# A gated mix of linear-memory attention and a SwiGLU layer on one core: seven weight operands made in four pieces, and loads, splits and two down groups on other beats

## The chip, the core and the metric

The kernel runs on one core of a Trainium2 chip. The metric is the device time of one execution in microseconds (us). Three runs before the change gave 1719.92, 1721.14 and 1722.72, with a median of 1721.14. TensorE is called PE below, its weight loads PEld, VectorE DVE, ScalarE ACT, GpSimd POOL, and the engine whose queue issues every DMA SP. Each engine works its own queue in the order in which the program was written. The kernel places every instruction by hand, and no scheduler moves any.

## The reference

```python
x = A_x                                            # 1 x 2048 x 576
g = sigmoid((x * gate_w).sum(-1, keepdims=True))
a = attention_with_memory(x, wq, wk, wv, beta) @ wo  # 32 heads of 18, 4 segments of 512 rows
b = (silu(x @ w_gate) * (x @ w_up)) @ w_down       # 576 -> 4608 -> 576
return g * a + (1 - g) * b
```

In each segment of 512 rows the attention is causal softmax within the segment. It is mixed per head, by `sigmoid(beta)`, with a linear-attention read of a memory that the earlier segments have filled. All inputs and the output are float32.

## The kernel before, in words

**Precision by splitting.** A float32 operand is held as two tiles of the type fp32r. The high one is ACT's copy of the number (an `activation` with `Copy`). The low one is DVE's difference of the number and the high one (`tensor_sub`). A product is then three matmuls: high by high, high by low, low by high. This making of a high and a low is called a split.

**Three stretches of the program.** First, up to about 219 us, the projections q, k, v and the memory. Then the long middle: 72 turns, in which the gate and up products of the feed-forward layer, its down products and the softmax attention are interleaved. Last, from about 1628 us, the output stage: the attention result times `wo`, the gate, and the down groups that are left.

**A turn.** The feed-forward layer is worked in two halves of the rows (two segments each) and 36 tiles of 128 hidden features, so 72 turns (`seq`, the loop over `pos`). In a turn gate and up of one feature tile for 1024 rows are computed as a 2x2 by 2x2 block product with seven multiplications in place of eight (Strassen's scheme, in Winograd's form). The seven products are the calls `seven(t, j)` for j = 0 to 6. Each is six matmuls of 512 columns with a weight operand `ops[j]` and an x operand `XO[j]` (L1027), and one for the last rows of the 576 (L1030). In a product the first two matmuls read the high of the weight operand, the third reads the low.

- Weight operands j = 0, 3 and 6 are plain blocks of the weights (a11, a12, a22). j = 1, 2, 4 and 5 are sums and differences of blocks that POOL makes (`total`, L265).
- After product 2 DVE adds a bank and a row (L1096). After product 4 ACT copies a bank (L1103) and DVE adds (L1104). Then ACT applies silu (L1106 for the first half of the rows, after a load of its table, and L1108 for the second). After product 6 DVE multiplies (L1112 and L1113), and that gives the hidden tile, which is split into `hh` and `hl` for the down product.

**Beats.** Between the products stand eight calls of `tick()`, the beats 0 to 7 of the turn: beat 0 after product 0, and so on, 5 and 6 together after product 5, 7 after product 6. A beat first runs what was put off to it (`due`), then down groups if there are any (`SHARE`), then steps of the attention (`att_gen`). A number of 8 or more in a plan's table is a beat of the next turn: 8 is its beat 0.

**Down groups.** Hidden tiles are taken in threes (`CH`). In each third turn 16 groups of 9 matmuls (L870) are issued, of 320 or 256 columns, two or three in each of the beats 2 to 7, so such a turn takes about 31 us, against about 17 and 12 for the two others.

**Who makes the weight operands.** `w_make(half, f)` plans in turn f - 1 what turn f needs: the sums on POOL, the highs on ACT (`HIGH` gives the beat, L269), the lows on DVE (`LOW`, L272). Each of the seven operands is a tile of its own of 128x512 (high and low, 256 each) from a pool of seven buffers. For the first two turns the operands are also written to DRAM (L275) and fetched again at the start of the second half (`w_fetch`, L713), because the weights are the same.

**The change of halves.** In the last turn of the first half (number 35) and ten further beats (`BREAK`) the x operands of the second half are loaded (`LOADS`), combined on POOL (`SUMS`) and split (`PARTS`) by `x_second`. Four of its eight loads lie in buffers of the weight operands.

**The output stage.** A row tile is transposed, multiplied by `wo` in two column halves (14 matmuls each, `products`, L160), and after each half one down group is issued (`downs(1)`). The first down groups there read the hidden tile of the very last turn.

## Time and profile before

| what | value |
|---|---|
| median of three runs | 1721.14 us |
| the profiled execution's own time | 1722.04 us |
| its span | 1720.3 us |
| PE busy | 1705.2 us (99%) |
| DVE busy | 1362.3 us (79%) |
| ACT busy | 1084.6 us (63%) |
| POOL busy | 937.9 us (55%) |
| granted PE clock | 1.00 |

A timeline row has the start in us from the span's beginning, the duration, the engine, the line, the operation, out<-in, shape and count. In brackets stand the idle time before it and what ended that. A row of the groups has the busy time, the mean duration of one in ns, and the idle time before. A row of the waits has the total, the number and the longest. A row of the windows has the stretch, its length, each engine's busy time with its count, the granted clock, the DMA share and GB/s. Matmuls of 512 columns are shown with 0.39 us each, but in a run of them one starts every 0.23 us (six in 1.52 us), since they overlap. DVE's instructions overlap by about 0.08 us in the same way.

### The profile page before, as it was taken

The numbers are of one execution on the slowest core, as the hardware profiler recorded it, in microseconds if no ns is written. First come the engines' busy times: TensorE is split into PE (matmuls) and PEld (weight loads), VectorE is DVE, ScalarE is ACT, GpSimd is POOL, SyncE is SP. The second block draws the span as 40 slices with busy tenths as digits, with TensorE's granted clock in tenths as the row PEclk, the third lists the DMA queues.
The fourth block names the chain that finished last, engine by engine and source line by source line (L and its number), as shares of the span: only waits on it lengthen the run. The fifth ranks groups of instructions, "written<-read, shape, count | busy, mean of one in ns | idle before, by whom it ended". The sixth has DMA issues, their size and how long they took to land.

```text
span 1720.3 us, 34819 instructions
## 1 busy us (share of the span) xinstructions
PE 1705.2 (99%) x11868; PEld 1479.8 (86%) x11868; DVE 1362.3 (79%) x3231; ACT 1084.6 (63%) x2123; POOL 937.9 (55%) x1194
## 2 busy tenths in 40 slices
PE   9999999999999999999999999999999999999999
PEld 7899978888888888888888788888888888888899
DVE  6557588888888889888889777787787788788655
ACT  7666576775776677567666756665666576566411
POOL 4434546666665655656566555565555555555311
PEclk9999999999999999999999999999999999999999
DMA  8654499998998898997979986787778677767633
GB/s 282 235 186 140 162 310 186 224 228 178 218 230 197 180 216 203 183 209 195 201 159 256 289 172 145 178 183 162 151 180 188 142 164 181 170 131 167 191 120 136
DMA packets 524002, 328.05 MB, mean 191 GB/s; under 512 B 411184, under 2 KB 460336, under 8 KB 523824
## 3 DMA queue, kind: packets, MB, share of 16 engines
q1 hardware_dynamic: 523824, 325.83, 78.0%
q8 instruction: 93, 1.52, 0.4%
q14 instruction: 85, 0.70, 0.1%
HBM read 165.76 MB, written 76.09 MB: 141 GB/s over the span
## 4 chain that ended last, share of the span: by engine, by line
PE 84%; DVE 7%; ACT 3%; issue 2%; DMA 2%; POOL 1%; SPq 0%; DVEq 0%; ACTq 0%; POOLq 0%
PE bank L1027 33%; PE bank L870 26%; PE bank L160 10%; PE bank L1030 5%; PE bank L728 4%; PE bank L776 2%; PE bank L777 1%; PE bank L415 1%; DVE hl L972 1%; DVE scr L734 1%; PE bank L461 1%; DVE dw L972 1%; DVE p L760 1%; PE bank L351 1%; DVE xo L138 1%
## 5 line engine op out<-in xcount | busy, mean ns | idle before, releaser
L761 POOL TENSOR_TENSOR p<-pe,p 128x512 f16<-128x512 f32 x320 | 378.4, 1182 | 417.0 <-DVE p L760 399.9
L870 PE MATMUL bank<-dw,hh 128*128 128x320 f32 (+1 forms) x2304 | 487.1, 304 | 1.5 <-DVE ya L880 1.5
L870 PEld LDWEIGHTS bank<-dw,hh 128*128 128x128 f32 x2304 | 381.1, 189 | 13.9 <-DVE ya L880 3.3
L746 ACT ACTIVATE pe<-bank,mb 128x512 f32<-128x512 f32 (+3 forms) x512 | 247.9, 526 | 196.2 <-DVE mb L734 183.1
L870 PE MATMUL bank<-dw,hl 128*128 128x320 f32 (+1 forms) x1152 | 340.6, 296 | 1.4 <-DVE hl L138 1.4
L734 DVE CUSTOM_DVE_ANT_0 scr<-bank,cm 128x512 bf16<-128x512 f32 (+3 forms) x512 | 246.5, 481 | 6.8 <-PE bank L728 0.2
L880 DVE TENSOR_TENSOR ya<-bank,ya 128x320 f32<-128x320 f32 x352 | 158.2, 453 | 77.8 <-PE bank L870 77.0
L870 PEld LDWEIGHTS bank<-dw,hl 128*128 128x128 f32 x1152 | 217.9, 189 | 1.9 <-DVE hl L138 1.9
L1030 PE MATMUL bank<-xr,rh 128*128 128x512 f32 x504 | 196.3, 390 | 0.0
L754 POOL TENSOR_SCALAR_AFFINE_SELECT pe<-pe 128x256 f32<-128x256 f32 (+1 forms) x320 | 151.6, 474 | 52.1 <-ACT pe L746 42.6
L760 DVE CAST p<-pe 128x512 f16<-128x512 f32 x320 | 160.6, 502 | 0.0
L265 POOL TENSOR_TENSOR ws<-raw 128x256 f32<-128x256 f32 x140 | 116.3, 831 | 16.1 <-DMA raw<-in_wf_dram 8.4
L728 PE MATMUL bank<-kst,qst 108*128 108x512 bf16 (+3 forms) x512 | 124.6, 305 | 0.3 <-DMA kst<-stk 0.2
L972 DVE TENSOR_TENSOR hl<-row,hh 128x512 fp32r<-128x512 f32 x120 | 108.4, 903 | 8.9 <-ACT hh L971 8.5
L1030 PEld LDWEIGHTS bank<-xr,rh 128*128 128x128 f32 x504 | 94.6, 188 | 20.4
L1104 DVE TENSOR_TENSOR row<-bank,row 128x512 f32<-128x512 f32 x72 | 49.7, 690 | 62.6 <-ACT bank L1103 62.5
L746 ACT ACT_TABLE_LOAD x69 | 88.5, 1283 | 10.8 <-DVE mb L734 9.8
L1089 ACT ACTIVATE bank<-bank 128x512 f32<-128x512 f32 x72 | 41.9, 582 | 79.8 <-PE bank L1030 76.7
L1106 ACT ACT_TABLE_LOAD x71 | 91.1, 1283 | 1.3
L1099 ACT ACTIVATE row<-bank 128x512 f32<-128x512 f32 x72 | 43.2, 600 | 71.5 <-PE bank L1030 71.3
L265 POOL TENSOR_TENSOR ws<-raw,ws 128x256 f32<-128x256 f32 x70 | 58.8, 840 | 49.9 <-DVE wo__22504 L272 9.7
L1103 ACT ACTIVATE bank<-bank 128x512 f32<-128x512 f32 x72 | 42.2, 587 | 65.5 <-PE bank L1030 65.1
(2170 smaller groups left out, 4123.1 us busy)
## 6 DMA issues: line engine op xcount, KB each, us to landing
raw<-in_wf_dram SPq DMA_DIRECT2D x140, 256.0 KB
rh<-rc SPq DMA_DIRECT2D x72, 336.0 KB
dc<-dw SPq DMA_DIRECT2D x36, 576.0 KB
dw<-dc SPq DMA_DIRECT2D x36, 576.0 KB
stk<-q SPq DMA_DIRECT2D x32, 384.0 KB
draw<-in_wd_dram SPq DMA_DIRECT2D x36, 288.0 KB
rc<-rt SPq DMA_DIRECT2D x42, 224.0 KB
vd<-vps SPq DMA_DIRECT2D x8, 912.0 KB
```

Source lines behind the costliest of these rows:

```text
L160: nc.tensor.matmul(t, st[n], mv[n], start=(n == 0), stop=(n == 13))
L265: (nc.gpsimd.tensor_sub if sub else nc.gpsimd.tensor_add)(src[j], p(), q())
L728: nc.tensor.matmul(t[:, c:c + w], qs[:KR, pr, P * i:P * i + P], ks[:KR, pr, 0:w], start=True, stop=True)
L734: nc.vector.tensor_tensor_reduce(scr[:, :w], t[:, c:c + w], cm[:, L - w:L], -SCALE, 3.0e38, OP.add, OP.min, m[:, k:k + 1])
L746: nc.scalar.activation(pe[:, c:c + w], t[:, c:c + w], AF.Exp, bias=m[:, k:k + 1], scale=SCALE)
L754: nc.gpsimd.affine_select(d, d, pattern=pat, compare_op=OP.is_ge, fill=0.0, base=0, channel_multiplier=1)
L760: nc.vector.tensor_copy(p[:, 0], pe)
L761: nc.gpsimd.tensor_sub(p[:, 1], pe, p[:, 0])
L870: nc.tensor.matmul(ts[m], p, q[:, cs], start=(n == 0), stop=(n == 3 * CH - 1))
L880: nc.vector.tensor_add(ya[:, i, cs], t, ya[:, i, cs])
L1027: nc.tensor.matmul(t, w[:, p, z], x[z][:, q], start=first and n == 0, stop=False, skip_group_check=True)
L1030: nc.tensor.matmul(t, rem[:, RPOS[j]], XR[j], start=False, stop=True, skip_group_check=True)
```

## The change

Three things are altered together.

1. The seven weight operands of a turn are made in four pieces: the operands (0, 3) in one tile, (1, 2) in one, (4, 6) in one, and 5 alone (`PAIRS`). A pair has one ACT copy and one DVE difference of 128x512 where there were two of 128x256. Each piece has one buffer, of the same total size as the seven before. The pairs are possible because a11 and a12 lie side by side in the raw tile `g`. The sums 1 and 2 now lie side by side in `ws`, and sum 4 is written over a21, beside a22. The beats of highs and lows are:

| operand | high before | high now | low before | low now | product at |
|---|---|---|---|---|---|
| 0 | 2 | 4 | 5 | 6 | 8 (after beat 7) |
| 3 | 7 | 4 | 8 | 6 | after 10 |
| 1 | 3 | 3 | 6 | 7 | after 8 |
| 2 | 3 | 3 | 7 | 7 | after 9 |
| 4 | 7 | 8 | 9 | 10 | after 11 |
| 6 | 9 | 8 | 11 | 10 | after 14 |
| 5 | 8 | 9 | 10 | 11 | after 12 |

   The copies to and from DRAM go by the same four pieces (512 KB for a pair, 256 KB before for one operand).
2. In `x_second` the loads, sums and splits stand on other beats, and four of the loads lie in `ws` and in the pieces (4, 6) and 5.
3. In the output stage the first two down groups are issued together: both groups' matmuls for the first two hidden tiles, and then both groups' for the last one (`down_parts`).

```diff
-HIGH = (2, 3, 3, 7, 7, 8, 9)
-LOW = (5, 6, 7, 8, 9, 10, 11)
+PAIRS = ((0, 3), (1, 2), (4, 6), (5,))
+HIGH = (4, 3, 8, 9)
+LOW = (6, 7, 10, 11)
...
-PARTS = ((1, 0, 0), (4, 0, 1), (10, 1, 0), (11, 1, 5), (12, 1, 3), (13, 0, 5), (13, 1, 1), (14, 1, 4), (15, 1, 2),
-         (17, 0, 2), (17, 1, 6), (18, 0, 3), (20, 0, 4), (22, 0, 6))
-FIRST = (9, 10, 11, 15, 17, 17, 19)
+PARTS = ((2, 0, 0), (4, 0, 1), (10, 1, 0), (11, 1, 5), (12, 1, 3), (13, 0, 5), (13, 1, 1), (14, 1, 4), (15, 1, 2),
+         (16, 0, 2), (17, 1, 6), (17, 0, 3), (18, 0, 4), (20, 0, 6))
+FIRST = ((9, 10, 18, 15), (4, 3, 8, 6))
...
-        def high(j):
-            ops[j] = op_tile()
-            nc.scalar.activation(ops[j][:, 0], src[j], AF.Copy)
-
-        def low(j):
-            nc.vector.tensor_sub(ops[j][:, 1], src[j], f32(ops[j][:, 0]))
...
+        def high(n):
+            tile_of[n] = op_tile(n)
+            op_views(ops, n, tile_of[n])
+            nc.scalar.activation(halves(n, 0), flat(n), AF.Copy)
+
+        def low(n):
+            nc.vector.tensor_sub(halves(n, 1), flat(n), f32(halves(n, 0)))
...
-        for j in range(7):
-            todo += [(HIGH[j], lambda j=j: high(j)), (LOW[j], lambda j=j: low(j))]
+        for n in range(4):
+            todo += [(HIGH[n], lambda n=n: high(n)), (LOW[n], lambda n=n: low(n))]
             if half == 0 and f < KEPT:
-                todo.append((LEAD + j + 3, lambda j=j: keep(j)))
+                todo.append((LOW[n] + 1, lambda n=n: keep(n)))
...
-                    downs(1)
+                    if n == 1 and hf == 0:
+                        down_parts([groups.pop(0) for _ in range(2)], CH - 1, CH)
+                    else:
+                        downs(1)
```

The queue of DVE at the end of turn 26 (two turns without down groups have gone by), before the change. `wo__10209`, `wo__10239` and `wo__10241` are the operands 0, 1 and 2 of turn 27; `dw` is the split of a down weight.

```order
L272 TENSOR_TENSOR wo__10209<-raw,wo__10209 128x256
L972 TENSOR_TENSOR dw<-draw,dw 128x576
L272 TENSOR_TENSOR wo__10239<-ws,wo__10239 128x256
L1112 TENSOR_TENSOR row<-bank_10250,row 128x512
L1113 TENSOR_TENSOR row<-row 128x512
L272 TENSOR_TENSOR wo__10241<-ws,wo__10241 128x256
L272 TENSOR_TENSOR wo__10299<-raw,wo__10299 128x256
```

The same place now (L997/L998 are the split of before's L971/L972, L1147 and L1148 its L1112 and L1113, L297 the low; `woa` is the pair (0, 3), `wob` the pair (1, 2)):

```order
L998 TENSOR_TENSOR dw<-draw,dw 128x576
L297 TENSOR_TENSOR woa__9946<-raw,woa__9946 128x512
L1147 TENSOR_TENSOR row<-bank_9942,row 128x512
L1148 TENSOR_TENSOR row<-row 128x512
L297 TENSOR_TENSOR wob__9933<-ws,wob__9933 128x512
L139 TENSOR_TENSOR hl<-row,hh 128x512
```

The low of operand 0 now stands behind the split of `dw` and is one instruction with that of operand 3. The low of operand 1 has moved from ahead of the two multiplications to behind them, and is one with that of operand 2. The lows of operands 3 and 4, at the beginning of the next turn, are gone from there.

The queue of ACT between product 3 and the silu of the same turn, before:

```order
L1099 ACTIVATE row<-bank_10145 128x512
L269 ACTIVATE wo__10239<-ws 128x256
L269 ACTIVATE wo__10241<-ws 128x256
L1103 ACTIVATE bank_10250<-bank_10143 128x512
L971 ACTIVATE dw<-draw 128x576
L746 ACTIVATE pe<-bank_10222,mb_2325 128x128
L746 ACTIVATE pe<-bank_10222,mb_2325 128x384
L1106 ACT_TABLE_LOAD
L1106 ACTIVATE row<-row 128x512
```

The same place now (L1138 is the copy of before's L1103, L1141 the silu of its L1106, L772 the exponential of its L746):

```order
L1134 ACTIVATE row<-bank_9844 128x512
L294 ACTIVATE wob__9933<-ws 128x512
L1138 ACTIVATE bank_9942<-bank_9842 128x512
L294 ACTIVATE woa__9946<-raw 128x512
L997 ACTIVATE dw<-draw 128x576
L772 ACTIVATE pe<-bank_9916,mb_2325 128x128
L772 ACTIVATE pe<-bank_9916,mb_2325 128x384
L1141 ACT_TABLE_LOAD
L1141 ACTIVATE row<-row 128x512
```

The high of operand 0 stood earlier in the turn, and now stands, as that of the pair (0, 3), between the copy and the silu.

More of the change, by code (lines that the diff above doesn't have):

```diff
@@ L231, in gated_mix, with op_tile, op_flat, op_home @@
     wraw_of, wops, rhs = {}, {}, []
-    def op_tile():
-        return wop.tile([P, 2, 2, P], F32R, name="wo_")
+    def op_tile(g, shape=None, dtype=F32R):
+        n = len(PAIRS[g])
+        return wop.tile(shape or [P, 2, n, 2, P], dtype, name=f"wo{'abcd'[g]}_", bufs=1)
+    def op_flat(t):
+        return f32(t).rearrange("p a j k n -> p (a j k n)")
+    def op_home(f, g):
+        return wc[f, :, 8 * P * g:8 * P * g + 4 * P * len(PAIRS[g])]
+    def op_views(ops, g, t):
+        for i, j in enumerate(PAIRS[g]):
+            ops[j] = t[:, :, i]
     def r_block(h, o):
@@ L255, in r_fetch, with w_make @@
         nc.sync.dma_start(f32(rhs[f % 2][:96]).rearrange("p j n -> p (j n)"), rc[f // 4, :, f % 4])
-    def w_make(half, f, LOW=LOW):
+    def w_make(half, f):
         g, u = wraw_of.pop(f)
@@ L709, in w_fetch, with one @@
             ops = wops[1, f] = [None] * 7
-            def one(j):
-                ops[j] = op_tile()
-                nc.sync.dma_start(f32(ops[j]).rearrange("p a k n -> p (a k n)"), wc[f, j])
-            return [(j + 2 if f else FIRST[j], lambda j=j: one(j)) for j in range(7)]
+            def one(n):
+                t = op_tile(n)
+                op_views(ops, n, t)
+                nc.sync.dma_start(op_flat(t), op_home(f, n))
+            return [(FIRST[f][n], lambda n=n: one(n)) for n in range(4)]
         kp = pool(ast, "kp", 2, side="right")
@@ L994, in x_second @@
         def x_second(new, rest):
-            r = {}
+            r, pair = {}, []
             todo = []
```

45 lines of the change are left out of this document (32 added, 13 removed).

## The prediction, made before the changed kernel was run

> **What bounds the kernel now.** I read the engines' busy shares first, then two windows (the busy times stand in the order PE, PEld, DVE, ACT, POOL), and then what PE and PEld wait for.
>
> ```profile
> span 1720.3 us, 34819 instructions
> PE 1705.2 (99%) x11868; PEld 1479.8 (86%) x11868; DVE 1362.3 (79%) x3231; ACT 1084.6 (63%) x2123; POOL 937.9 (55%) x1194
> 215.00:845.00 630.00, 624.89 (x4449) 532.74 (x4449) 548.92 (x1319) 428.65 (x838) 386.24 (x517) 1.00 0.92 209
> 960.00:1625.00 665.00, 664.64 (x4716) 574.02 (x4715) 524.38 (x1284) 423.57 (x820) 363.28 (x464) 1.00 0.75 171
> ```
>
> PE is the bound in every stage, at the full clock, and the change takes no matmul from it. What the change can gain is only what PE now waits; what it can lose has no such limit. In the second half of the turns (960 to 1625) PE is idle for 0.4 us of 665: a new wait there is a loss in full. DVE is 87% busy in the first half (548.92 of 630), so work reaches PE from there with little to spare.
>
> ```profile
> PE bank L1027 <- ACT bank L1103: 2.4, 5, 0.9
> PE bank L1027 <- DVE bank L1096: 1.7, 4, 0.7
> PE bank L870 <- DVE hl L138: 1.4, 2, 1.2
> PE bank L1027 <- DVE xo L138: 0.5, 2, 0.3
> PE bank L1027 <- DVE wo__3704 L272: 0.3, 1, 0.3
> PEld bank L1027 <- ACT bank L1103: 6.3, 10, 1.3
> PEld bank L1027 <- DVE bank L1096: 5.0, 9, 1.1
> ```
>
> A wait shows at the weight load and again, shorter, at the matmul. PE waits for the bank that ACT copies (L1103), the bank that DVE adds (L1096), late x and hidden lows (L138), and only once for a weight operand's low (L272). All of it together is some 14 us.
>
> **Part 1, the pairs: what is saved.** The first row is DVE's window for the lows alone, the second ACT's for the highs; the others are the same operation at 512 elements.
>
> ```profile
> 219.20:1628.10 1408.90, 281.64 (x489) 1.00 0.84 193
> 219.20:1628.10 1408.90, 190.30 (x487) 1.00 0.84 193
> L972 DVE TENSOR_TENSOR hl<-row,hh 128x512 fp32r<-128x512 f32 x120 | 108.4, 903 | 8.9 <-ACT hh L971 8.5
> L971 ACT ACTIVATE hh<-row 128x512 fp32r<-128x512 f32 x120 | 75.3, 628 | 0.9 <-DVE row L1113 0.9
> 732.49 0.68 DVE L972 TENSOR_TENSOR hl<-row,hh 128x512 fp32r<-128x512 f32 x1
> ```
>
> A low of 256 takes 281.64/489 = 0.58 us in the mean, a high 190.30/487 = 0.39. Seven lows are 4.03 us a turn; three of 512 (0.90) and one of 256 are 3.29, so DVE saves 0.74 us a turn. ACT goes from 2.74 to 2.27 and saves 0.47. Over some 70 turns that is 52 us of DVE and 33 of ACT, but neither is the bound, so this is worth only the waits that it shortens.
>
> **Part 1: what comes later.** A low must be there at the third matmul of its product, 0.45 us after the first (two starts of 0.23). The pair (1, 2) is now made behind both multiplications, and operand 1 is wanted a product earlier than operand 2 was, which had that place. I take two windows. The first is the end of turn 13, without a split of `dw`; `wo__6442`, `wo__6473` and `wo__6475` are operands 0, 1 and 2.
>
> ```profile
> 488.64 0.39 PE L1030 MATMUL bank<-xr,rh 128*128 128x512 f32 x1
> 490.55 1.46 PE L1027 MATMUL bank<-xo,wo__6473 128*128 128x512 f32 x5
> 489.13 0.69 DVE L1112 TENSOR_TENSOR row<-bank,row 128x512 f32<-128x512 f32 x1 [0.53 <-PE bank L1030]
> 489.74 0.68 DVE L1113 TENSOR_TENSOR row<-row 128x512 f32<-128x512 f32 x1
> 490.34 0.42 DVE L272 TENSOR_TENSOR wo__6475<-ws,wo__6475 128x256 fp32r<-128x256 f32 x1
> 485.69 0.58 ACT L1103 ACTIVATE bank<-bank 128x512 f32<-128x512 f32 x1 [0.44 <-PE bank L1030]
> 488.18 0.63 ACT L1106 ACTIVATE row<-row 128x512 f32<-128x512 f32 x1
> ```
>
> DVE here waits for PE's product 6 (489.03), then multiplies twice. The pair's low begins at 490.34 at the earliest and takes 0.68: ready at 491.02, wanted at 490.55 + 0.45 = 491.00. So even an idle DVE is 0.02 late. But ACT has the high of (0, 3) between L1103 and the silu now: 0.63 less an overlap of 0.1 is 0.52 more. L1103 itself waited for PE, so nothing earlier makes this good; the silu ends at 489.33 in place of 488.81, L1112 starts at about 489.36, and the low is ready at 491.25, 0.25 late. With the mean 0.90 for 512 elements it is 0.47. Bounds 0.02 and 0.47; I take 0.20, near the row's own 0.25, since in some turns ACT has room before the silu.
>
> The second window is the end of turn 26, with the split of `dw` (the place whose order is shown above).
>
> ```profile
> 740.09 1.59 PE L1027 MATMUL bank<-xo,wo__10209 128*128 128x512 f32 x6
> 741.75 1.69 PE L1027 MATMUL bank<-xo,wo__10239 128*128 128x512 f32 x6
> 739.61 0.81 DVE L272 TENSOR_TENSOR wo__10209<-raw,wo__10209 128x256 fp32r<-128x256 f32 x1
> 740.35 0.95 DVE L972 TENSOR_TENSOR dw<-draw,dw 128x576 fp32r<-128x576 f32 x1
> 741.22 0.96 DVE L272 TENSOR_TENSOR wo__10239<-ws,wo__10239 128x256 fp32r<-128x256 f32 x1
> 742.11 0.68 DVE L1112 TENSOR_TENSOR row<-bank,row 128x512 f32<-128x512 f32 x1
> 743.54 0.41 DVE L272 TENSOR_TENSOR wo__10241<-ws,wo__10241 128x256 fp32r<-128x256 f32 x1
> 740.22 0.63 ACT L1106 ACTIVATE row<-row 128x512 f32<-128x512 f32 x1
> ```
>
> DVE works without a gap. Operand 0 falls away at 739.61, `dw` takes its place until 740.48, and the pair (0, 3) is ready at 741.16, wanted at 740.09 + 0.45 = 740.54: 0.62 late. With 0.90 it is 0.84; where DVE arrives 0.4 earlier, by the shorter lows before, it is 0.2. L1112 then starts about 741.1 (also the silu's time, 740.85 and a part of the 0.52), the pair (1, 2) begins 1.2 to 1.4 later and is ready at 743.0 to 743.2, wanted at 742.20 plus the 0.62: another 0.2 to 0.4. Bounds 0.2 and 1.2; I take 0.7.
>
> How many turns: in every third turn the 16 down groups lie between the beats 2 and 7, and the next turn's operands have time. Of the 47 others, 11 in the first half have `dw` in this place, as in the second window (weights' lows are not made again in the second half); 35 count as the first, and the start of the second half is fetched. 35 x 0.20 = 7.0 and 11 x 0.7 = 7.7: **14.7 us**, between 35 x 0.02 + 11 x 0.2 = 2.9 and 35 x 0.47 + 11 x 1.2 = 29.7. What waits behind PE is the next product and all that follows.
>
> The pair (4, 6) and operand 5 come one beat later than 4 and 5 did, and the pair is 0.27 longer than one low. Ahead of them two lows are gone. No row shows these being waited for: 0 to 13 us (0.27 in 47 turns); I take 1.5.
>
> **Part 1: what PE is spared.** L1096 has two lows fewer ahead of it (those of operands 3 and 4, 1.16 us by the mean): of its 5.0 us I take 3.0 as gone, 0 to 5.0. L1103 keeps its 6.3: ahead of it on ACT stand 0.52 in place of two times 0.3, at the same place behind the same sum. I take 0, between 2 gained and 2 lost. In turn 0 the wait comes from a write to DRAM:
>
> ```profile
> 232.96 0.42 ACT L269 ACTIVATE wo__2722<-ws 128x256 fp32r<-128x256 f32 x1 [2.25 <-DMA wc<-wo__2473]
> 227.75 1.17 SPq L275 DMA_DIRECT2D wc<-wo__2473  x1
> ```
>
> ACT may not overwrite operand 2 until the write of 256 KB, issued at 227.75, has landed at 232.96. The pair's write is 512 KB, issued from the same place in SP's queue, and ACT's high of the next pair stands at the same beat, ahead of L1103 again: 0 to 1.5 us more, I take 0.5. SP has fewer issues than before, which were hidden anyway.
>
> **Part 2, x on other beats.**
>
> ```profile
> 912.44 0.69 DVE L138 TENSOR_TENSOR xo<-raw,xo 128x512 fp32r<-128x512 f32 x1 [1.59 <-ACT xo L137]
> 915.35 1.65 PE L1027 MATMUL bank<-xo,wo__12823 128*128 128x512 f32 x6 [0.71 <-DVE bank L1096]
> 951.80 1.43 PE L1027 MATMUL bank<-xo,wo__13331 128*128 128x512 f32 x5 [0.29 <-DVE xo L138]
> 955.51 1.43 PE L1027 MATMUL bank<-xo,wo__13380 128*128 128x512 f32 x5 [0.24 <-DVE xo L138]
> ```
>
> In turn 35 DVE waits 1.59 us for ACT at the first x split, with L1096 queued behind it; the split now stands behind L1096, and that wait of PE goes (counted in the 3.0). The x operands 4 and 6 come one and two beats sooner, so the other two waits, 0.5 us, go. The fetch of pair (4, 6), at beat 18, must wait on SP for a split at beat 17, and everything in SP's queue with it: 0 to 2 us if it lands after product 4 begins; I take 0, since the same pool of operands was issued at the same place before.
>
> **Part 3, two down groups together.**
>
> ```profile
> 1633.06 0.41 PE L870 MATMUL bank<-dw,hl 128*128 128x320 f32 x1 [1.21 <-DVE hl L138]
> 1635.36 0.40 PE L870 MATMUL bank<-dw,hh 128*128 128x256 f32 x2
> 1635.72 0.40 PE L870 MATMUL bank<-dw,hh 128*128 128x256 f32 x2
> ```
>
> Three matmuls of 256 columns take 0.36 us (1635.36 to 1635.72), so six of the second group put 0.7 us of work into the wait of 1.21. Gain 0.7; nothing to lose.
>
> **The sum**, on the profiled execution's 1722.04: 14.7 + 1.5 + 0.5 - 3.0 - 0.5 - 0.7 = 12.5, so 1734.5. That execution lies 0.9 over the median of 1721.14, so the forecast is **1733**, about 0.7% slower.
>
> **Rivals.** *Faster: the saved fixed cost reaches PE.* If DVE is early by the 0.74 us a turn where it matters, so that no pair is late, PE keeps the gains and part of the L1103 waits: 3.0 + 0.5 + 0.7 + 4 = 8 us, 1713, or some 1717 with half of it. For it: DVE is 87% busy in the first half, and the second window's delay is all queue. Against it: the first window has no queue in it, only PE, two multiplications and one low. It decides from a mean lateness under 0.09 us in 47 turns (4.2/47). Chance 0.16. The Trainium skill, page "VectorE: DVE Perf Modes", section on the TRN2 errata, states this rule: an instruction from SBUF pays a fixed latency once, so tiles of 512 and more are to be preferred. By it alone the change would gain; the trace agrees on the price of the instruction (0.68 for 512 against twice 0.42), but what is asked here is when the first half of the pair is ready.
>
> *No change: the two lists cancel.* Lateness of 0.05 to 0.13 in the 47 turns, as an idle DVE with the silu in time would have it: 2.4 to 6 us, less 4.2 gained: 1719 to 1723. Chance 0.14.
>
> *Much slower: DVE meets POOL each time.* The same form of low takes 0.42 and 0.96 in one window. If the pairs stretch like that, the upper bounds hold: 29.7 + 5 - 3 = 32, 1753. For it: the mean of 0.90 in 120 cases. Against it: nearly every window would have to be the worst one. From about 1745 on I give it 0.08.
>
> **How the numbers follow.** The likeliest, slower by its waits at products 0 and 1, has 0.62 and by itself a range of 1726 to 1745. With 0.08 for much slower, slower has 0.70. A measurement of this kernel tells about 0.2% (3.4 us) from no change; the three chances are bounded there. The range for 8 in 10 takes in the even case and the upper edge of the faster: 1717 to 1745.
>
> **What would show it.** In the profile after: PE and PEld waits for L297 (`woa`, `wob`) in most turns of two in three, some 10 to 20 us in all, in the second half too; the wait on L1131 (before's L1096) smaller than 5.0; silu 0.5 later against L1138; the wait at 1633 down to about 0.5; those at 951 and 955 gone. Wrong it is if the pairs (0, 3) and (1, 2) are ready before the third matmul with DVE idle, or if PE's busy time in 960 to 1625 shows no new gap.

## The result, and the profile after

The changed kernel takes 1759.8 us (median of four runs, 1758.5 to 1762.5) against 1721.9 for the kernel before in the same comparison. The ratio is 1.0223, with a 95% interval of 1.0211 to 1.0236. I had forecast 1733, with a range of 1717 to 1745. The sign was right and the size was not: 38 us lost, where I had worked out 12.5.

The head of the page of the profiled execution after (own time 1762.54), and two windows of the turns, with the busy times in the order PE, PEld, DVE, ACT, POOL:

```profile
span 1760.7 us, 34418 instructions
PE 1719.8 (98%) x11868; PEld 1474.9 (84%) x11868; DVE 1308.6 (74%) x3021; ACT 1064.2 (60%) x1913; POOL 938.9 (53%) x1194
215.00:845.00 630.00, 611.56 (x4266) 513.09 (x4265) 508.21 (x1184) 410.26 (x724) 375.31 (x502) 1.00 0.89 204
960.00:1660.00 700.00, 687.73 (x4834) 584.81 (x4832) 511.27 (x1213) 421.24 (x730) 374.59 (x475) 1.00 0.74 169
```

The clock is 1.00 as before, and PE has as many matmuls as before. DVE is 53.7 us less busy (1362.3 before), and yet PE now idles 18.4 us of 630 in the first window (5.1 before) and 12.3 us of 700 in the second (0.4 of 665 before). That is 25 us more. PE's busy time also rose, from 1705.2 to 1719.8 for the same matmuls, so idle time shows only a part of the loss. What PE and PEld wait for, some of the largest rows and that of the bank which DVE adds (L1131, before's L1096):

```profile
PE bank L1062 <- ACT bank L1138: 3.4, 6, 1.3
PE bank L1062 <- DMA woa__13034<-wc: 2.1, 1, 2.1
PE bank L1062 <- DVE wob__22052 L297: 1.6, 1, 1.6
PE bank L1062 <- DVE woa__7348 L297: 1.4, 1, 1.4
PE bank L1062 <- DVE wod__6412 L297: 1.1, 1, 1.1
PEld bank L1062 <- ACT bank L1138: 6.9, 9, 1.7
PEld bank L1062 <- DVE wob__22052 L297: 2.0, 1, 2.0
PEld bank L1062 <- DVE bank L1131: 1.7, 4, 0.8
```

Each late low is a row of its own, since each turn's tile has its own number. Added up over PEld's rows, the lows of (1, 2), `wob`, make PEld wait 24.3 us in 39 turns, operand 5, `wod`, 17.4 in 22, (0, 3), `woa`, 10.4 in 12, and (4, 6), `woc`, 3.1 in 10. Before, the lows had some 2 us between them. The wait for the bank that DVE adds fell from 5.0 to 1.7, the waits for late x at 951 and 955 are gone, and so is that of 1.21 in the output stage.

For what follows I use one more reading. For every two matmuls in a row I take the distance of their starts less the median distance of all pairs of the same two shapes, and add up what exceeds 0.06 us, by the product in which the waiting matmul stands. A part of these sums is there in every kernel; what counts is the difference of two columns. All in us; the names of the versions are explained below. The sums are from one execution each, whose own time stands in the last row.

| PE held up in | before | change | first two lows early | operand 5 early | all lows early | highs and lows earlier |
|---|---|---|---|---|---|---|
| product 0 | 2.9 | 14.1 | 4.2 | 17.2 | 4.0 | 4.3 |
| product 1 | 6.9 | 24.1 | 7.9 | 27.3 | 8.7 | 8.7 |
| product 5 | 5.2 | 18.9 | 20.7 | 5.2 | 5.2 | 5.2 |
| product 6 | 8.0 | 8.3 | 6.9 | 12.2 | 9.0 | 6.6 |
| everywhere | 72.2 | 110.4 | 86.3 | 105.6 | 79.2 | 72.4 |
| time, median | 1721.9 | 1759.8 | 1735.9 | 1756.5 | 1726.9 | 1721.0 |
| time of this execution | 1722.0 | 1762.5 | 1736.8 | 1756.5 | 1730.5 | 1722.1 |

So the loss lies where the prediction had put it, at products 0 and 1, and at a third place that it had nearly written off: product 5.

### The profile page after: what moved, and what is told of

Read it like the earlier page. It is cut to its first block, busy times and chain, and to the rows that moved or that the text cites. A ratio compares the mean times of both kernels' runs of the same rounds, so it can differ in the third digit from the quotient of the medians.

```text
span 1760.7 us, 34418 instructions
## 1 busy us (share of the span) xinstructions
PE 1719.8 (98%) x11868; PEld 1474.9 (84%) x11868; DVE 1308.6 (74%) x3021; ACT 1064.2 (60%) x1913; POOL 938.9 (53%) x1194
## 3 DMA queue, kind: packets, MB, share of 16 engines
q8 instruction: 94, 1.54, 0.4%
## 4 chain that ended last, share of the span: by engine, by line
PE 63%; DVE 7%; ACT 6%; issue 5%; POOL 3%; DMA 3%; SPq 1%; DVEq 0%; POOLq 0%; ACTq 0%
PE bank L896 25%; PE bank L1062 24%; PE bank L1065 4%; PE bank L161 3%; PE bank L754 3%; PE bank L802 2%; PE bank L803 1%; ACT L1141 1%; ACT pe L772 1%; DVE hl L998 1%; POOL p L787 1%; POOL ws L283 1%; DVE scr L760 1%; DVE p L786 1%; DMA raw<-in_wf_dram 1%
## 5 line engine op out<-in xcount | busy, mean ns | idle before, releaser
L896 PE MATMUL bank<-dw,hh 128*128 128x320 f32 (+1 forms) x2304 | 486.8, 304 | 1.0 <-DVE ya L906 1.0
L896 PEld LDWEIGHTS bank<-dw,hh 128*128 128x128 f32 x2304 | 381.3, 189 | 13.2 <-DVE ya L906 1.8
L772 ACT ACTIVATE pe<-bank,mb 128x512 f32<-128x512 f32 (+3 forms) x512 | 246.7, 527 | 202.6 <-DVE mb L760 188.5
L896 PE MATMUL bank<-dw,hl 128*128 128x320 f32 (+1 forms) x1152 | 340.4, 295 | 0.0
L906 DVE TENSOR_TENSOR ya<-bank,ya 128x320 f32<-128x320 f32 x352 | 157.2, 453 | 89.7 <-PE bank L896 88.1
L896 PEld LDWEIGHTS bank<-dw,hl 128*128 128x128 f32 x1152 | 217.9, 189 | 0.0
L998 DVE TENSOR_TENSOR hl<-row,hh 128x512 fp32r<-128x512 f32 x120 | 107.2, 894 | 35.2 <-ACT hh L997 34.9
L772 ACT ACT_TABLE_LOAD x69 | 88.5, 1283 | 13.3 <-DVE mb L760 12.3
L1131 DVE TENSOR_TENSOR bank<-bank,row 128x512 f32<-128x512 f32 x72 | 50.3, 699 | 47.6 <-PE bank L1065 26.4
L1138 ACT ACTIVATE bank<-bank 128x512 f32<-128x512 f32 x72 | 42.1, 584 | 69.8 <-PE bank L1065 69.7
L161 PE MATMUL bank<-xo,qhi 128*128 128x512 f32 x264 | 83.2, 396 | 0.9 <-ACT vps L425 0.9
```

The source lines that it names most:

```text
L161: nc.tensor.matmul(t, st[n], mv[n], start=(n == 0), stop=(n == 13))
L772: nc.scalar.activation(pe[:, c:c + w], t[:, c:c + w], AF.Exp, bias=m[:, k:k + 1], scale=SCALE)
L896: nc.tensor.matmul(ts[m], p, q[:, cs], start=(n == 0), stop=(n == 3 * CH - 1))
L906: nc.vector.tensor_add(ya[:, i, cs], t, ya[:, i, cs])
L998: defer(k + 1, lambda: nc.vector.tensor_sub(lo, src, f32(hi)))
```

## The experiments

The theory: the lows stand too near to their products (`LOW`), and that is what PE waits for. The rival: a low of 512 elements is too long a piece, wherever it stands. Each version is the changed kernel with the edit shown, unless the text says that it is the kernel before. The times of the kernel before in the five comparisons were 1721.3 to 1721.9.

### The beats of the lows

**All four a beat earlier.**

```diff
-LOW = (6, 7, 10, 11)
+LOW = (5, 6, 9, 10)
```

> The changed kernel with the lows of all four groups at the beats 5, 6, 9, 10 in place of 6, 7, 10, 11, nothing else. Theory 'late lows': PE waits for the first product of each group because the subtraction stands too near to that product; the changed kernel's waits at products 0, 1 and 5 grew by about 8.9, 17.5 and 13.8 us, so most of these 40 us should go: 1722 to 1732 us, and faster than before by a few us if the saved DVE time counts. Rival 'large pieces': a subtraction of 512 elements holds DVE too long wherever it stands, and the waits only move to the bank that DVE adds (L1131) and to x: 1748 us or more.

1726.9 us, ratio 1.0033 (1.0021 to 1.0045), within the theory's range. 33 of the 38 us are gone with four numbers. PEld's waits in its trace:

```profile
PEld bank L1062 <- ACT bank L1138: 7.8, 10, 1.2
PEld bank L1062 <- DVE bank L1131: 5.5, 9, 1.3
PEld bank L896 <- DVE ya L906: 5.3, 8, 1.1
PEld bank L1062 <- DVE wob__2982 L297: 0.6, 1, 0.6
```

The lows are hardly waited for any more. The wait for L1131 is back at 5.5: the low of (4, 6), at beat 9, now stands ahead of that sum on DVE again. (L896 is the matmul of the down groups, before's L870, and L906 the sum on DVE that takes their result.)

**Operand 5 alone, and the first two pairs alone.**

```diff
-LOW = (6, 7, 10, 11)
+LOW = (6, 7, 10, 10)
```

> The changed kernel with the low of operand 5 alone at beat 10 in place of 11 (directly behind that of the pair 4, 6). Theory 'late lows': the growth of 13.8 us at product 5 goes, the rest stays: 1746 to 1750 us. Rival 'large pieces': operand 5 is late because the pair (4, 6) is long and stands ahead of it, so that a beat earlier gains little: 1755 us or more.

```diff
-LOW = (6, 7, 10, 11)
+LOW = (5, 6, 10, 11)
```

> The changed kernel with the lows of the pairs (0, 3) and (1, 2) at the beats 5 and 6 in place of 6 and 7, the others as changed. Theory 'late lows': the growth of 26.4 us at products 0 and 1 goes, that at product 5 stays: 1732 to 1737 us. Rival 'large pieces': the subtraction of 512 elements now stands ahead of the two multiplications with which the turn ends, these come later and with them the next products: 1750 us or more.

The first two pairs: 1735.9 us, ratio 1.0085 (1.007 to 1.01), so 23.9 us gained, as the theory had it, and nearly all of the growth at products 0 and 1 is gone. Operand 5: 1756.5, ratio 1.0205 (1.019 to 1.0221), only 3.3 gained (the interval overlaps that of the changed kernel), although its whole wait at product 5 is gone from the table. That is the rival's figure without its reason: operand 5 is no longer late, and the time is hardly better. Turn 14 shows where the rest went; first the changed kernel, DVE and PE:

```profile
503.70 0.68 DVE L297 TENSOR_TENSOR woc__6384<-raw,woc__6384 128x512 fp32r<-128x512 f32 x1
504.30 1.23 DVE L998 TENSOR_TENSOR hl<-row,hh 128x512 fp32r<-128x512 f32 x1
505.45 0.42 DVE L786 CAST p<-pe 128x512 f16<-128x512 f32 x1
506.59 0.79 DVE L297 TENSOR_TENSOR wod__6412<-wt,wod__6412 128x256 fp32r<-128x256 f32 x1
507.43 1.21 PE L1062 MATMUL bank<-xo,wod__6412 128*128 128x512 f32 x4 [1.13 <-DVE wod__6412 L297]
```

Then the version with operand 5 a beat earlier, the same turn:

```profile
502.71 0.96 DVE L297 TENSOR_TENSOR wod__6412<-wt,wod__6412 128x256 fp32r<-128x256 f32 x1
504.19 1.52 PE L1062 MATMUL bank<-xo,wod__6412 128*128 128x512 f32 x6
508.79 1.20 PE L1062 MATMUL bank<-xo,woa__6474 128*128 128x512 f32 x4 [0.81 <-DVE woa__6474 L297]
```

At beat 11 the low of operand 5 stands behind the split of the hidden tile, a cast and the maxima, 2.9 us after that of (4, 6). A beat earlier it directly follows it and product 5 runs through. But the low of (0, 3) for the next turn does not come earlier by as much as PE now does, so PE waits 0.81 there, where it did not wait in the changed kernel: of 1.13 gained, 0.3 is kept.

**The same beat without the pairs.** In the kernel before, one number:

```diff
-LOW = (5, 6, 7, 8, 9, 10, 11)
+LOW = (5, 6, 7, 8, 9, 11, 11)
```

> The kernel before with one number changed: the low of operand 5 at beat 11 in place of 10, where the change has it. In the changed kernel the steps to product 5 grew by 13.8 us, but moving this low back there gained only 3.3 us, since 4 us came up again at product 6 and 6 us at products 0 and 1 of the next turn. Theory 'waits stand in for each other': in the changed kernel PE is held up by DVE at three places, and what one of them gives up the next takes; alone, in a kernel without the others, the same beat costs nearly its whole wait: 1731 to 1742 us. Rival 'the wait at product 5 is free': PE only waits there for what it would wait for later anyway: 1722 to 1726 us.

1724.35 us, ratio 1.0015 (1.0006 to 1.0024), against 1721.48 in this comparison: 2.9 us, the rival's figure. The sum of product 5 grew by 6.9 (5.2 to 12.0), while those of the products 4, 6, 0 and 1 each shrank a little. So even alone, a good part of a wait at product 5 is a wait that PE would have had later. My theory that it costs nearly its whole wait there fell; a price of about 3 us for this beat stands from both sides.

**How much room a low needs.**

```diff
-LOW = (6, 7, 10, 11)
+LOW = (5, 6, 10, 10)
```

> The changed kernel with the lows at the beats 5, 6, 10, 10: pairs (0, 3) and (1, 2) and operand 5 a beat earlier, the pair (4, 6) where the change has it. With all four a beat earlier the waits at product 4 were 13.8 us (7.8 in the changed kernel), with the first two alone 10.4. Theory 'one beat of room': a low needs a whole beat between it and its product, but no more, and a low that stands earlier than that only pushes back the bank that DVE adds: about 3 us under the 1726.9 of all four, 1722 to 1725 us. Rival 'pairs cost by themselves': the pairs' length still shows, whichever beats are taken: 1726 us or more.

1732.7 us, ratio 1.0068 (1.0055 to 1.0081): 5.8 slower than with (4, 6) at beat 9. I had expected that low to be in the way when early, and it is the other way round. PEld's waits in this kernel:

```profile
PEld bank L1062 <- ACT bank L1138: 10.0, 11, 2.0
PEld bank L1062 <- DVE bank L1131: 2.5, 7, 0.6
```

The low was in the way: the wait for L1131 is 2.5 in place of 5.5. But in its place PEld waits 4.5 us in 14 turns for (4, 6) itself, and the sum of product 4 is little changed (6.5 against 7.0). By the sums, what is late besides is product 6 (11.1 against 9.0), which waits for the bank that ACT copies, and products 0 and 1 (15.7 against 12.7).

**The beats without the pairs.** The kernel before, seven operands apart, on the changed kernel's beats:

```diff
-HIGH = (2, 3, 3, 7, 7, 8, 9)
-LOW = (5, 6, 7, 8, 9, 10, 11)
+HIGH = (4, 3, 3, 4, 8, 9, 8)
+LOW = (6, 7, 7, 6, 10, 11, 10)
...
-                start = w_make(0, 0, LOW[:3] + (7,) + LOW[4:])
+                start = w_make(0, 0)
```

> The kernel before, its seven operands apart as they were, but with highs and lows on the beats of the changed kernel: highs of 0 and 3 at beat 4, of 1 and 2 at 3, of 4 and 6 at 8, of 5 at 9; lows of 0 and 3 at 6, of 1 and 2 at 7, of 4 and 6 at 10, of 5 at 11. x and the output stage as before. Theory 'late lows': the beats alone cost, so this is slower too, 1740 to 1765 us (operand 0 and operand 1 are the first of their pair, which spares them about 0.3 us each, but DVE has 0.74 us more a turn). Rival 'large pieces': 1722 to 1730 us.

1751.6 us, ratio 1.0177 (1.0162 to 1.0192). Against the kernel before in the same comparison (1721.5), 30 us are lost with the beats alone, and no pair is in this kernel. The rival of the large pieces is left with some 8. But the loss does not stand at the same places: here the sums of products 0 and 1 grew by 11.9 and that of product 5 by 21.5, in the changed kernel by 28.4 and 13.7. So the agreement of the totals does not say that each place is late for the same reason.

### The parts inside the lateness

**The high of (0, 3) and the silu.** I had priced it at 0.52 us of delay for the multiplications behind the silu. First I moved it behind the silu:

```diff
-HIGH = (4, 3, 8, 9)
+HIGH = (5, 3, 8, 9)
```

> The changed kernel with the high of the pair (0, 3) a beat later on ACT (beat 5 in place of 4), so that it stands behind the silu and not ahead of it; the lows as changed. My prediction's theory: the silu that this high delays by 0.52 us delays the multiplications and with them the lows of (0, 3) and (1, 2), some 0.2 us in 35 turns: 5 to 9 us of the 38.6 go, 1751 to 1755 us. Rival 'the silu is not waited for' (in the changed kernel the copy-to-silu time grew by 0.38 us in the median and the silu-to-multiplication time shrank by 0.43): 1758 to 1762 us, or more if the high now keeps the copy of the bank waiting.

1803.0 us, ratio 1.0473 (1.0459 to 1.0488), which neither side had expected. ACT of this version, and the largest wait for the high:

```profile
1338.51 1.28 ACT L1141 ACT_TABLE_LOAD   x1
1339.80 0.63 ACT L1141 ACTIVATE row<-row 128x512 f32<-128x512 f32 x1
1340.34 0.58 ACT L1143 ACTIVATE row<-bank 128x512 f32<-128x512 f32 x1
1340.82 0.62 ACT L294 ACTIVATE woa__17460<-raw 128x512 fp32r<-128x512 f32 x1
PE bank L1062 <- ACT woa__7368 L294: 2.4, 1, 2.4
```

Behind the table load and two activations the high comes some 2.3 us later, and product 0 needs it with its first matmul, not with the third: PE waits 34.6 us in 39 places for highs of `woa`. The silu's own price could not be read from it, so I moved the high the other way, to beat 3, ahead of the copy:

```diff
-HIGH = (4, 3, 8, 9)
+HIGH = (3, 3, 8, 9)
```

> The changed kernel with the high of (0, 3) at beat 3 in place of 4, ahead of that of (1, 2) and of the bank copy, so that it no longer stands between the copy (L1138) and the silu (L1141). If the silu's delay of 0.5 us makes the pairs (0, 3) and (1, 2) late, as my prediction had it, half or more of the 26 us at products 0 and 1 goes: 1740 to 1750 us. If the silu is not what the multiplications wait for, or if the high now delays the bank copy by the same 0.6 us, 1756 to 1766.

1753.5 us, ratio 1.0187 (1.0173 to 1.0201), between the two expectations: 6.3 gained, the sums of products 0 and 1 down by 8.1. The group of the first multiplication, with DVE's idle time before it, in the kernel before, in the changed kernel, and in this version:

```profile
L1112 DVE TENSOR_TENSOR row<-bank,row 128x512 f32<-128x512 f32 x72 | 49.6, 689 | 31.6 <-PE bank L1030 25.3 <-ACT row L1106 3.6 <-ACT wo__11024 L269 1.6
```

```profile
L1147 DVE TENSOR_TENSOR row<-bank,row 128x512 f32<-128x512 f32 x72 | 49.7, 691 | 46.1 <-PE bank L1065 28.2 <-ACT row L1141 14.0 <-ACT row L1143 2.8
```

```profile
L1147 DVE TENSOR_TENSOR row<-bank,row 128x512 f32<-128x512 f32 x72 | 49.7, 690 | 37.2 <-PE bank L1065 32.4 <-ACT row L1141 2.6 <-ACT dw L997 0.8
```

DVE's wait for the silu rose from 3.6 to 14.0 us, and falls to 2.6 with the high out of the way. So the silu's delay was real, but it is a quarter of the loss at products 0 and 1, not its main part.

**The length of the low.** Each pair's low as two subtractions of 256, directly behind each other, on the changed kernel's beats:

```diff
-            nc.vector.tensor_sub(halves(n, 1), flat(n), f32(halves(n, 0)))
+            for i in range(len(PAIRS[n])):
+                t, s = tile_of[n], src[n][:, 2 * i:2 * i + 2]
+                nc.vector.tensor_sub(t[:, 1, i], s, f32(t[:, 0, i]))
```

> The changed kernel with each long low made as two subtractions of 256 elements directly behind each other, on the same beats: first halves 0, 1 and 4, then 3, 2 and 6. Highs, tiles and transfers stay merged. If the long low is what is late, since its first half is not ready before the second, operands 0 and 1 are ready 0.3 to 0.5 us sooner in 46 turns, less DVE's 0.74 more a turn: 1745 to 1752 us, like the kernel with single operands on these beats (1751.6). If it is the place behind the multiplications alone, 1758 to 1766.

1753.0 us, ratio 1.0182 (1.0168 to 1.0195): 6.7 gained, between the two expectations. The length counts, but only as much as the silu.

**Both together.**

```diff
-HIGH = (4, 3, 8, 9)
+HIGH = (3, 3, 8, 9)
...
-            nc.vector.tensor_sub(halves(n, 1), flat(n), f32(halves(n, 0)))
+            for i in range(len(PAIRS[n])):
+                t, s = tile_of[n], src[n][:, 2 * i:2 * i + 2]
+                nc.vector.tensor_sub(t[:, 1, i], s, f32(t[:, 0, i]))
```

> The changed kernel with both edits: the high of (0, 3) at beat 3 (alone 6.3 us gained) and the long lows in two subtractions on the same beats (alone 6.7 us gained). If they are separate causes, the gains add: 1746 to 1748 us. If each only takes a part of the same lateness, which the other gives back, 1750 to 1753.

1750.3 us, ratio 1.0164 (1.0148 to 1.0179): 9.5 gained, not 13.0. They overlap by 3.5. What is left, 29 us, is about what the beats cost with seven single operands (30).

**The highs of (4, 6) and 5.** No term of my sum.

```diff
-HIGH = (4, 3, 8, 9)
+HIGH = (4, 3, 7, 8)
```

> The changed kernel with the highs of (4, 6) and of operand 5 a beat earlier (7 and 8 in place of 8 and 9), the lows as changed. With early lows, highs and lows a beat earlier gave 1721.0 against 1726.9. If the highs did that, by standing behind and not ahead of ACT's copies of the next turn, some 6 us go here as well: 1751 to 1755. If it was the lows at 8 and 9, nothing changes here: 1758 to 1761.

1755.3 us, ratio 1.0197 (1.0183 to 1.0211): 4.5 gained, about the first figure. By the sums 2.6 went at product 0 and 1.3 at product 5, and no row shows PE waiting for one of these highs.

### Pairs with nothing late

**Highs and lows earlier.**

```diff
-HIGH = (4, 3, 8, 9)
-LOW = (6, 7, 10, 11)
+HIGH = (4, 3, 7, 8)
+LOW = (5, 6, 8, 9)
```

> The changed kernel with lows at the beats 5, 6, 8, 9 and the highs of the last two groups at 7 and 8 (8 and 9 in the change), so a beat earlier still than the kernel with all lows early (1726.9, waits for lows gone; what is left there are the banks that ACT copies, 7.8 us at the weight load, and that DVE adds, 5.5). Theory 'lateness is used up': with no low awaited any more, a further beat gains nothing: 1725 to 1729. Rival 'earlier is better still': 1718 to 1724. Third possibility, the lows now stand ahead of the bank's sum and delay it: 1729 to 1740.

1721.0 us, ratio 0.9998 (0.9989 to 1.0007): all of the loss is gone, the rival's figure and not that of my theory. Two windows of its trace:

```profile
215.00:845.00 630.00, 624.40 (x4441) 531.48 (x4440) 530.94 (x1222) 420.29 (x741) 399.96 (x517) 1.00 0.91 209
960.00:1625.00 665.00, 664.27 (x4750) 574.01 (x4749) 513.11 (x1181) 416.18 (x717) 375.38 (x463) 1.00 0.75 171
```

DVE has 18 us less work in the first window and 11 in the second than before the change (548.92 and 524.38), and PE is as busy as it was (624.89 and 664.64). The saved DVE time buys nothing. Compared with the version with all lows early, the sums fell by 2.4 at product 6 and by 3.7 outside the products: PEld's wait for the bank that ACT copies went from 7.8 to 5.4, and the down groups' wait for DVE's sum (L906) from 5.3 to 1.8. What PE waited for there was not a low but ACT's copy and DVE's sum.

By the Trainium skill (page "VectorE: DVE Perf Modes", the section on the TRN2 errata), which advises tiles of 512 and more because the fixed latency is paid once per instruction, the pairs should be the better form; the trace agrees on the saving and shows that it is no time of the kernel.

**Lows apart, at the old beats, highs and tiles in pairs.** The highs at 4, 3, 8, 9, the low of operand j at beat 5 + j:

```diff
+        def low_one(j):
+            n, i = next((n, p.index(j)) for n, p in enumerate(PAIRS) if j in p)
+            t, s = tile_of[n], src[n][:, 2 * i:2 * i + 2]
+            nc.vector.tensor_sub(t[:, 1, i], s, f32(t[:, 0, i]))
...
-            todo += [(HIGH[n], lambda n=n: high(n)), (LOW[n], lambda n=n: low(n))]
+            todo.append((HIGH[n], lambda n=n: high(n)))
+            todo += [(5 + j, lambda j=j: low_one(j)) for j in PAIRS[n]]
...
```

> The changed kernel with its four tiles, four highs and four transfers, but the lows as seven subtractions of 256 elements again, operand j at beat 5 + j as before the change. With the four long lows a beat earlier the time was 1726.9, some 7 us over the 1719.6 that I take for the kernel before with parts 2 and 3 (1721.9 less 1.8 and 0.4). Theory 'the first half waits for the second': those 7 us are the price of the long lows, of which no half is ready before the whole; then this takes 1719 to 1722. Rival 'the merged highs': the high of (0, 3) must wait for the buffer of operand 3 and stands ahead of the silu, and that is the 7 us: 1725 to 1729.

1726.2 us, ratio 1.0028 (1.0019 to 1.0038), the figure of the rival "the merged highs" and that of the long lows a beat early (1726.9). The time is the same, but the loss stands elsewhere: product 6 has 12.3 us here and 9.0 there, and its wait is for the bank that ACT copies (L1144 is L1138 in this version):

```profile
PEld bank L1068 <- ACT bank L1144: 10.7, 10, 2.2
```

So this run does not show that the length of an early low costs nothing. It shows that single lows at the old beats do not bring back the last 5 us while the highs stand at 4, 3, 8, 9. That leaves the highs at 8 and 9 as the likely place: the version above has them a beat earlier, with the last two lows, and is as fast as the kernel before.

**The fetch at the start of the second half, and the high of (0, 3), once more.** The first has `FIRST[1]` as (3, 3, 8, 6) in place of (4, 3, 8, 6), the second `HIGH` as (3, 3, 7, 8) besides.

> Pairs with highs at 4, 3, 7, 8 and lows at 5, 6, 8, 9 (1721.0 us) and the fetch of the pair (0, 3) for the first turn of the second half at beat 3 in place of 4, so that its 512 KB land sooner. In that kernel the trace has one wait of 1.8 us at this place. If the fetch was only issued late, 1719.0 to 1719.8 us, as good as the kernel before with parts 2 and 3 (1720.0); if the transfer is slow because of what else the queues move at that time, 1720.5 to 1721.5.

> Pairs with highs at 3, 3, 7, 8, lows at 5, 6, 8, 9 and the first fetch at beat 3. With the high of (0, 3) at 4 this takes 1721.15 us. If the silu's delay costs there too, 1716 to 1719, faster than both kernels. If the lows that stand early enough have already taken its cost away, 1720 to 1722, no difference to the kernel before.

1721.15 us, ratio 0.9999 (0.999 to 1.0008), and 1721.4, ratio 1.0001 (0.9992 to 1.0009). Neither moves the time: with early lows the silu's delay no longer shows, and at the fetch PE's wait of 1.7 us for (0, 3) is gone from the trace while one of 0.8 for the fetched pair (4, 6) of the turn before is there, which is too little to be told in the time. (This fetch is for the second turn of the second half, `FIRST[1]`, and not for the first.) Merged operands were not faster than single ones in any version.

### Parts 2 and 3 alone, in the kernel before

The first has the `LOADS`, `SUMS` and `PARTS` of the change and nothing else; the second the output stage's edit (`down_parts` for the first two groups); the third both.

> The kernel before with the second part alone: loads, sums and splits of x on the changed kernel's beats, weights' operands apart and on their own beats. Theory of the prediction: the two late x (0.5 us) and the wait behind the x split in turn 35 (0.7) go: 0.5 to 1.2 us gained, 1720.3 to 1721. By the waits at product 4, which fell by 3.6 us in the changed kernel: if it is x that did it, 1718 us; if it is the two lows fewer ahead of the bank's sum, 1721 us.

> The kernel before with the third part alone: the first two down groups of the output stage begun together. My prediction: 0.7 us gained, as six matmuls of 0.12 go into a wait of 1.21. The changed kernel's trace has that wait gone altogether (1.38 to 0 by its steps): 1.2 to 1.5 us gained, 1720.0 to 1720.3. Both are within what tells from no change; the profile's row at this place decides.

> The kernel before with parts 2 and 3 of the change and without part 1: x on the new beats (alone 1720.2 against 1721.9) and the two down groups begun together (alone 1721.5). If the two gains add, 1719 to 1720 us, faster by 0.1 to 0.15 per cent, which five rounds can just tell. If not, 1720 to 1722.

1720.2 us, ratio 0.9989 (0.998 to 0.9998); 1721.5, ratio 0.9997 (0.9988 to 1.0006); 1720.0, ratio 0.9993 (0.9984 to 1.0002). The beats of x gain about 0.1%. The down groups take most of the wait away; in their version the first low is met like this:

```profile
1630.48 0.46 PE L870 MATMUL bank<-dw,hh 128*128 128x320 f32 x2
1631.07 0.42 PE L870 MATMUL bank<-dw,hl 128*128 128x320 f32 x1
```

0.59 us between these two starts, 0.29 of it for the two matmuls, where 1.21 was waited before. In the whole time this is too little to be told. Both together have the lowest time found, but their interval takes in no change, and they are not faster than the beats of x alone by more than the noise.

## Why the prediction was wrong, and where it was right

**The bound.** Right. PE has the full clock, and it is PE's waits that make the loss, some two thirds of it as idle time in the two windows and most of the rest in a longer busy time of the same matmuls. The second half, with 0.4 us of room before, lost like the first.

**What is saved.** For DVE right: 52 us forecast, 53.7 measured. For ACT too high: 33 forecast, 20.4 measured. That neither is the bound was shown by the version that keeps the savings and is no faster than before. The rival "the saved fixed cost reaches PE" fell with it. (The sum itself gives 1733.6; the forecast rounds it down.)

**The second window** (12 turns of the first half with the split of `dw`). Right in size: the sums of products 0 and 1 grew by 10.1 us there, 0.84 a turn, where I took 0.7 between 0.2 and 1.2.

**The first window** failed. I took 0.20 in 35 turns, 7.0 us; the growth in the other turns, without the 2.3 us of the late fetch, is 16.1, or 0.46 each in the mean, at the upper bound of 0.47. I had named the bound, and had chosen "near the row's own". Two windows of the changed kernel without a split of `dw` ahead of the low show what the chosen row left out. A good one:

```profile
1418.07 0.69 DVE L1147 TENSOR_TENSOR row<-bank,row 128x512 f32<-128x512 f32 x1 [1.29 <-PE bank L1065]
1418.67 0.68 DVE L1148 TENSOR_TENSOR row<-row 128x512 f32<-128x512 f32 x1
1419.27 0.69 DVE L297 TENSOR_TENSOR wob__18910<-ws,wob__18910 128x512 fp32r<-128x512 f32 x1
1419.39 1.36 PE L1062 MATMUL bank<-xo,wob__18910 128*128 128x512 f32 x4
```

The low is there at 1419.96, wanted at 1419.39 + 0.45 = 1419.84: 0.12 late. And a bad one, with POOL beside it:

```profile
1298.24 0.69 DVE L1147 TENSOR_TENSOR row<-bank,row 128x512 f32<-128x512 f32 x1 [0.24 <-ACT row L1141]
1298.85 1.26 DVE L1148 TENSOR_TENSOR row<-row 128x512 f32<-128x512 f32 x1
1300.03 0.68 DVE L297 TENSOR_TENSOR wob__17289<-ws,wob__17289 128x512 fp32r<-128x512 f32 x1
1300.77 0.50 PE L1062 MATMUL bank<-xo,wob__17289 128*128 128x512 f32 x1 [0.81 <-DVE wob__17289 L297]
1298.13 0.74 POOL L283 TENSOR_TENSOR raw<-raw 128x256 f32<-128x256 f32 x1
1298.82 0.74 POOL L283 TENSOR_TENSOR wt<-raw,ws 128x256 f32<-128x256 f32 x1
```

The second multiplication takes 1.26 in place of 0.68, beside POOL's sum for operand 5, and the low comes behind it. I had let the low itself grow, by the mean of 0.90, and kept the multiplication ahead of it at the 0.68 of my one window. The group's row of the kernel before had the warning, and after the change it is a little longer:

```profile
L1113 DVE TENSOR_TENSOR row<-row 128x512 f32<-128x512 f32 x72 | 59.2, 822 | 0.0
```

```profile
L1148 DVE TENSOR_TENSOR row<-row 128x512 f32<-128x512 f32 x72 | 62.0, 862 | 0.0
```

A mean of 0.82 over rows of 0.68 means that many are far longer: 22 of 72 took over 0.85 before, 27 of 72 after. Sorted by this multiplication, the 35 turns fall in two kinds. In 11 of them L1148 took over 1 us beside POOL, and the sums of products 0 and 1 grew by 10.1 us, 0.92 each. In the other 24 they grew by 4.5, 0.19 each, which is the size that I had taken, and more than half of these did not grow at all. (What is left of the 16.1 stands in turns 1 and 37.) So the term was wrong not in every turn but by leaving out the turns in which POOL runs beside the multiplication. This is read from the trace of one execution; no run moves POOL's sums, so it is not shown by experiment. The rival "DVE meets POOL each time" had this mechanism, at the wrong instruction and with too small a chance. The silu's part I had right as a mechanism: 6.3 us by the run that takes it away.

**The pair (4, 6) and operand 5** failed most for their size. I took 1.5 of 0 to 13, since no row showed these being waited for. PE's sum at product 5 grew by 13.7, and the steps back cost 3.2 for operand 5 (1735.9 to 1732.7) and 5.8 for (4, 6) (1732.7 to 1726.9): 9.0 in place of 1.5. The step that failed is taking the absence of a wait for room: in the kernel before a single beat later for operand 5 costs 2.9 us, and the prediction never looked at what stands in the beat that it lost.

**The highs at the beats 8 and 9** were missing from the sum. They are worth 4.5 us alone, where the prediction had nothing.

**What PE is spared.** The number was right (5.0 to 1.7, 3.3 for 3.0 forecast), and its reason holds for a part. Two versions that differ in the beat of the low of (4, 6) alone have 5.5 with this low ahead of L1131 and 2.5 with it behind. The beats of x alone take 5.0 to 3.6 in the kernel before, which my 3.0 had counted in. The last part, from 2.6 with the first two lows early to 1.7, goes with PE's lateness at products 0 and 1. L1138 was taken as unchanged and went from 6.3 to 6.9. In turn 0 I took 0.5 for the larger write; ACT waits 2.38 us for it, where it waited 2.25. What this did to PE was not separated:

```profile
234.00 0.63 ACT L294 ACTIVATE wob__2703<-ws 128x512 fp32r<-128x512 f32 x1 [2.38 <-DMA wc<-wob__2468]
```

**Part 2.** The two waits for x went, as forecast. The fetch of (4, 6) at beat 18 cost nothing, as forecast; another one did, that of (0, 3) for the second turn of the second half:

```profile
975.36 1.45 SPq L739 DMA_DIRECT2D woa__13034<-wc  x1
980.40 2.72 PE L1062 MATMUL bank<-xo,woa__13034 128*128 128x512 f32 x6 [2.14 <-DMA woa__13034<-wc]
```

**Part 3.** Right in kind. The wait of 1.21 is gone in the changed kernel's trace, where I took 0.7 of it as gained; in the time this is too little to be seen.

By undoing one thing after another, the loss from 1759.8 is: 23.9 for the lows of (0, 3) and (1, 2), 3.2 for that of operand 5, 5.8 for that of (4, 6), and 5.9 for the last two highs with one more beat for their lows. These steps follow each other; taken in another order they would come out otherwise, as the 6.3 and 6.7 that make 9.5 show. Against them stand 14.7 for the first, 1.5 for the two that follow, and nothing for the last. Three things stay open: how much of the 5.9 is the highs and how much the lows, why (4, 6) at beat 10 makes ACT's copy ahead of product 6 late, and how much of the loss would go if POOL's sums stood elsewhere.

## What to carry to other kernels

When pieces of work are merged, the merged piece is due at the earliest of its products, and its first half is not ready before the whole: look first at which beats this leaves, and only then at what one instruction less saves on an engine that is not the bound. A wait of zero in the profile does not say how much room there is; before a piece is moved later, list what stands ahead of it in the queue at its new place, with the group's mean for each duration and not with the row of one window. A wait that is taken away is worth only what the next wait does not take back (13.7 us gone at product 5 were 3.3 of the time), and a piece that no row shows as waited for can still be worth some us (4.5 for the last two highs). So the price of a move has to be measured in the time.

## What the runs showed of the hardware that I had not expected

DVE's multiplication with one input in PSUM (L1147) takes 0.68 to 0.69 us in all 72 turns, whatever POOL does. The one with both inputs in SBUF (L1148), of the same size, takes 0.68 in each turn in which no POOL instruction runs beside it, and up to 1.54 in the others. The two rows at 1298 show both within a microsecond, under the same kind of POOL instruction. The Trainium skill (page "SBUF — State Buffer", section "SBUF: two separate sides") says that a DVE instruction with two SBUF inputs and a POOL instruction that reads SBUF lock each other out of a pair of ports that they share, the one that comes first keeping it to its end. The trace agrees: the excess of 0.58 us in that row is less than the 0.74 of the POOL instruction that began 0.03 us before it. Where the multiplication began first, it kept its 0.68, and the sum on POOL, 0.74 in the row above, took 1.24:

```profile
697.71 0.68 DVE L1148 TENSOR_TENSOR row<-row 128x512 f32<-128x512 f32 x1
697.74 1.24 POOL L283 TENSOR_TENSOR wt<-raw,ws 128x256 f32<-128x256 f32 x1
```
